# A fixed, periodic order of instructions in place of a list scheduler, with PSUM banks used by halves, in an attention and soft-MoE kernel

## The chip, the cores and the metric

The kernel runs on one core of a Trainium2 chip. The metric is the device time of one execution, in microseconds; below it is called the time. A profiled execution gives a trace beside its time: the instructions of TensorE (PE, with its weight loads apart as PEld), VectorE (DVE), ScalarE (ACT), GpSimd (POOL) and SyncE (SP, which only issues transfers here), and the transfers.

## What is computed

```python
def _attn_ref(q, kv, w_sr):                  # q [4, 12288, 128], kv [4, 384, 32, 128]
    kv_pool = kv.reshape(B, H // r, r, W // r, r, C).mean(axis=(2, 4))     # r = 4
    kv_flat = kv_pool.reshape(B, -1, C) @ w_sr                             # 768 keys a batch
    k = v = kv_flat
    s = scale * (q @ k.transpose(0, 2, 1))
    a = np.exp(s - s.max(-1, keepdims=True))
    a /= a.sum(-1, keepdims=True) + 1e-09
    return a @ v
def _moe_ref(x, phi, w1, w2):                # x [49152, 128], 8 experts, 4 slots each
    logits = x @ phi                         # 32 slots
    d = np.exp(logits - logits.max(0, keepdims=True))
    d /= d.sum(0, keepdims=True) + 1e-09     # over all tokens
    slot_input = d.T @ x
    for e in range(E):
        slot_out[e] = np.maximum(slot_input[e] @ w1[e], 0.0) @ w2[e]
    c = np.exp(logits - logits.max(1, keepdims=True))
    c /= c.sum(1, keepdims=True) + 1e-09     # over the slots
    return c @ slot_out
```

`_moe_ref` gets the output of `_attn_ref`, flattened to 49152 tokens.

## The kernel before

**Tiling.** A tile is 128 queries. There are 384 tiles, 96 to a batch, in 48 groups of eight (`G`). The attention output x is never made: the logits are P @ (v phi), and the slots' inputs are (D^T P) @ v, where P holds the exponentials of the scores and D the exponentials of the logits with a running maximum over the tokens.

**Per tile** (`plan_tile`): `qk` makes the scores with six matmuls (high and low parts of q and k), `rmax` (VectorE) the negated row maximum, `pexp` (ScalarE) the exponentials and their row sum. The last 384 of the 768 columns go to float16 as a high half (`p_hi`, ScalarE) and a low half (`p_lo`, GpSimd), and `p_dma` has them transposed by a transfer that SyncE issues. The first 384 columns of a pair of tiles are transposed by VectorE (`ptr`). Every four tiles `q_hi` (ScalarE) and `q_lo` (GpSimd) split q.

**Per group** (`plan_logits`, `plan_group`): `la_mm` (three steps, LA below) and `lb_mm` (three, LB) add up the logits in two PSUM tiles, `lp` and `lq`; two copies on ScalarE (`l_ev`) bring them to SBUF, `l_sel` multiplies them with a selecting matrix into `psl`, `l_tr` (VectorE) transposes them into LL, `l_n` (GpSimd) divides by the row sums. `m_col`, `m_mm`, `m_red`, `m_run` make the maximum over tokens (VectorE, TensorE, VectorE), `d_sub`, `d_exp`, `d_mul` (GpSimd, ScalarE, GpSimd) make D, `t_mm` (four steps of a pair of tiles, T0 to T3 below) makes D^T P in `pst`, and `t_acc` adds it up. `c_max`, `c_sub`, `c_exp` prepare the last softmax; `c_sum`, `c_eps`, `c_rec`, `c_mul` finish it, group by group.

**Per batch:** the keys of the next batch come in by one plain load of SyncE and three accumulating loads of GpSimd (`kv_acc`) and two folding transfers (`kv_fold`), into the tail of LL. `kv_ops` then makes k, u = v phi and v (`k_mm`, `u_mm`, `u_t`, `v_mm` on TensorE and what empties them); `b_tr`, `b_sum`, `b_mm`, `b_acc` close a batch.

**Tail:** the weights are loaded, the experts run (`e_psi` to `e_fin`), and 32 chunks of 12 tiles are transposed (`o_tr`), multiplied (`o_mm`), copied (`o_ev`) and written out (`o_dma`).

**What sets the order.** Every step is an `op` of a `Plan`, with an engine, a cost, a priority in assumed time (`T0`: 2 us a tile), what it depends on, and the rings of buffers that it takes and uses. `Plan.emit` runs a list scheduler at build time over those costs: at each step the engine that can start first takes its best ready operation (`NEAR`, `HOLD` and the flag `hot` shade the choice). The outcome is the program order of TensorE, VectorE, ScalarE and GpSimd; each engine then works strictly in that order, and waits where an operand is not there. PSUM holds three tiles of two banks in the ring `s` (scores; also `lq`, `pu`) and one tile of two banks in the ring `m`, which `lp`, `psl`, `pg`, `pst` and the small products take in turn, one at a time.

Of the kernel before, what the change touches and what calls it, by code (L numbers as in the profile page):

```python
# [24 lines left out]

class Plan:
    LAG = 0.08
    NEAR = 0.12
    HOLD = 0.7

    def __init__(self, rings):
        self.cap = rings
# [12 lines left out]

    def emit(self):
        ops = self.ops
        inf = math.inf
        waits = [len(o[4]) for o in ops]
        nexts = [[] for _ in ops]  # L50
        for n, o in enumerate(ops):
            for d in o[4]:
                nexts[d].append(n)
        ready, avail = {}, {}
        for n, o in enumerate(ops):
            avail.setdefault(o[0], [])
            ready[n] = o[8]
            if waits[n] == 0:
                avail[o[0]].append(n)
        left = {key: len(u) for key, u in self.users.items()}  # L60
        part, freed, rings = {}, {}, {}
        free = dict.fromkeys(avail, 0.0)
        todo = len(ops)

        def acquire(n):
            t = 0.0
            want = {}
            for key in ops[n][6]:
                ring = key[0]
                held = rings.get(ring, ())  # L70
                want[ring] = want.get(ring, 0) + 1
                back = self.cap[ring] - want[ring] + 1
                if len(held) >= back:
                    t = max(t, freed.get(held[-back], inf))
            return t

        def best(e):
            found = []
            for n in avail[e]:
                t = acquire(n)  # L80
                if t < inf:
                    found.append((max(free[e], ready[n], t), ops[n][3], n))
# [945 lines left out]
```

## Time and profile before

| | us |
|---|---|
| median of 3 runs | 1182.01 (1180.49 to 1182.15) |
| profiled execution, its own time | 1180.24 |
| its span, first to last instruction | 1178.5 |
| TensorE, VectorE, ScalarE, GpSimd busy | 896.4, 779.6, 736.6, 660.5 |

The span is what the trace covers; the execution's own time has 1.7 us more around it. Busy time counts an engine's instructions, and not its waits or the issue of transfers. The ends of matmuls are modelled, so a matmul's listed length is longer than the step from one start to the next. The granted clock of TensorE is given as a share of 2.4 GHz: 1.00 is that level, 0.50 is 1.2 GHz.

### The profile page before, as it was taken

The numbers are of one execution on the slowest core, as the hardware profiler recorded it, in microseconds if no ns is written. First come the engines' busy times: TensorE is split into PE (matmuls) and PEld (weight loads), VectorE is DVE, ScalarE is ACT, GpSimd is POOL, SyncE is SP. The second block draws the span as 40 slices with busy tenths as digits, with TensorE's granted clock in tenths as the row PEclk, the third lists the DMA queues.
The fourth block names the chain that finished last, engine by engine and source line by source line (L and its number), as shares of the span: only waits on it lengthen the run. The fifth ranks groups of instructions, "written<-read, shape, count | busy, mean of one in ns | idle before, by whom it ended". The sixth has DMA issues, their size and how long they took to land. (4 is left out here: it accounts for less than half of the span.)

```text
span 1178.5 us, 32165 instructions
## 1 busy us (share of the span) xinstructions
PE 896.4 (76%) x12708; PEld 674.6 (57%) x12708; DVE 779.6 (66%) x1629; ACT 736.6 (63%) x1548; POOL 660.5 (56%) x893
## 2 busy tenths in 40 slices
PE   1738988878970976898874398988897988985893
PEld 0627776556750764676653277765675766763341
DVE  5617778567831865878760468786885787784492
ACT  1626888567840864878761458785885788773251
POOL 1428677456742754777761557675775777774000
PEclk9969999889985997999997699999998999998895
DMA  7797777365797753566587646875773766759299
GB/s 298 153 177 120 119 127 119 63 111 95 129 186 141 121 98 66 102 122 121 113 171 150 127 72 118 115 128 83 115 123 75 122 118 116 121 82 304 94 412 379
DMA packets 332262, 165.18 MB, mean 140 GB/s; under 512 B 309968, under 2 KB 310224, under 8 KB 331216
## 3 DMA queue, kind: packets, MB, share of 16 engines
q1 hardware_dynamic: 328368, 145.29, 59.0%
q0 software_dynamic: 3312, 17.70, 8.0%
q8 instruction: 100, 1.64, 0.6%
q14 instruction: 50, 0.41, 0.1%
q10 hardware_dynamic: 432, 0.15, 0.0%
HBM read 58.87 MB, written 25.17 MB: 71 GB/s over the span
## 5 line engine op out<-in xcount | busy, mean ns | idle before, releaser
L428 ACT ACTIVATE p<-s,nm 128x768 f32<-128x768 f32 x384 | 341.2, 889 | 199.6 <-DVE nm L420 199.0
L419 DVE TENSOR_REDUCE nm<-s 128x1 f32<-128x768 f32 x384 | 363.7, 947 | 145.6 <-PE s L415 145.1
L438 POOL TENSOR_TENSOR hl<-p,hl 128x384 f16<-128x384 f32 x384 | 353.4, 930 | 82.6 <-ACT hl L435 78.1
L413 PE MATMUL s<-khi,qhi 128*128 128x384 f32 x768 | 284.8, 371 | 64.1 <-ACT p L428 63.5
L414 PE MATMUL s<-klo,qhi 128*128 128x384 f32 x768 | 261.3, 340 | 0.0
L415 PE MATMUL s<-khi,qlo 128*128 128x384 f32 x768 | 261.3, 340 | 0.0
L435 ACT ACTIVATE hl<-p 128x384 f16<-128x384 f32 x384 | 200.8, 523 | 55.7 <-DMA pb<-hl 37.5
L413 PEld LDWEIGHTS s<-khi,qhi 128*128 128x128 f32 x768 | 146.8, 191 | 117.5 <-ACT p L428 84.1
L588 PE MATMUL pst<-p,D 128*32 128x192 f32 x3072 | 157.1, 364 | 74.0 <-POOL D L573 65.6
L450 DVE STREAM_TRANSPOSE pa<-p 128x768 f32<-128x768 f32 x192 | 183.3, 955 | 12.9 <-ACT p L428 12.7
L588 PEld LDWEIGHTS pst<-p,D 128*32 128x32 f32 x3072 | 106.6, 122 | 122.0 <-POOL D L573 78.7
L414 PEld LDWEIGHTS s<-klo,qhi 128*128 128x128 f32 x768 | 147.3, 192 | 0.5 <-issue 0.5
L415 PEld LDWEIGHTS s<-khi,qlo 128*128 128x128 f32 x768 | 146.6, 191 | 0.0
L393 POOL TENSOR_TENSOR qlo<-q,qhi 128x512 fp32r<-128x512 f32 x96 | 123.5, 1287 | 30.7 <-ACT qhi L389 30.5
L521 POOL TENSOR_TENSOR LL<-LL,ri 128x256 f32<-128x256 f32 x48 | 29.9, 623 | 128.5 <-DVE LL L507 128.5
L475 PE MATMUL lq<-pa,vu 32*32 32x256 f32 x2304 | 98.3, 390 | 1.5 <-ACT p L428 1.5
L475 PE MATMUL lp<-pa,vu 32*32 32x256 f32 x2304 | 97.3, 390 | 0.5 <-DVE acc L599 0.5
L389 ACT ACTIVATE qhi<-q 128x512 fp32r<-128x512 f32 x96 | 60.0, 625 | 33.5 <-PE s L414 22.1
L533 PE MATMUL pg<-ident,cm 128*128 128x128 f32 x96 | 24.0, 334 | 74.3 <-DVE cm L528 58.7
L428 ACT ACTIVATION_READ_ACCUMULATOR p<-s,nm 128x1 f32 x384 | 73.5, 191 | 0.0
L420 DVE TENSOR_SCALAR nm<-nm 128x1 f32<-128x1 f32 x384 | 59.0, 154 | 13.2
L475 PEld LDWEIGHTS lp<-pa,vu 32*32 32x32 f32 x2304 | 51.2, 103 | 27.6 <-issue 10.5
(121 smaller groups left out, 960.8 us busy)
## 6 DMA issues: line engine op xcount, KB each, us to landing
q<-qT SPq DMA_DIRECT2D x96, 256.0 KB, 3.1
outT<-o SPq DMA_DIRECT2D x32, 768.0 KB, 13.4
LL<-kvT POOLq DMA_DIRECT2D x9, 1536.0 KB, 11.0
LL<-kv SPq DMA_DIRECT2D x8, 768.0 KB, 11.4
pb<-hl SPq DMA_TRANSPOSE x384, 2.8
LL<-kvT SPq DMA_DIRECT2D x3, 1536.0 KB, 7.2
w_pa<-w SPq DMA_DIRECT2D x2, 1536.0 KB, 9.5
w_pb<-w SPq DMA_DIRECT2D x2, 1536.0 KB, 10.0
```

The costliest lines, as they stand in the source:

```text
L389: nc.scalar.activation(qsp[i][0], src, AF.Copy)
L393: nc.gpsimd.tensor_tensor(out=lo, in0=src, in1=hi.bitcast(F32), op=ALU.subtract)
L413: nc.tensor.matmul(s, hi[:, qc], khi[:, k], start=True, stop=False)
L414: nc.tensor.matmul(s, hi[:, qc], klo[:, k], start=False, stop=False)
L415: nc.tensor.matmul(s, lo[:, qc], khi[:, k], start=False, stop=True)
L419: nc.vector.tensor_reduce(out=NM[t], in_=S[t][:, :, :HK], axis=XY, op=ALU.max, negate=True)
L428: nc.scalar.activation(PP[t // 2][:, t % 2, :].rearrange("p (h n) -> p h n", h=2), S[t][:, :, :HK], AF.Exp, bias=NM.pop(t), scale=1.0, acc ...
L435: nc.scalar.activation(HL[t][:, 0, :], PP[t // 2][:, t % 2, KA:], AF.Copy)
L438: nc.gpsimd.tensor_tensor(out=HL[t][:, 1, :], in0=PP[t // 2][:, t % 2, KA:], in1=HL[t][:, 0, :], op=ALU.subtract)
L450: nc.vector.transpose(out=PA[g][:, :, o : o + 2, :].rearrange("p n a i -> p a n i"), in_=PP[k][:, :, :KA].rearrange("p a (n j) -> p a n j" ...
L475: nc.tensor.matmul(lp(g, c, r), VU[b][rows, kb, :], PA[g][rows, kb, :, :], start=(k == 0), stop=False, skip_group_check=True)
L588: nc.tensor.matmul(d["pst"][c * Q32 : (c + 1) * Q32, :KW], d["D"][:, t, :], pp[:, u, c * KW : (c + 1) * KW], start=(t == 0), stop=(t == G ...
```

## The change

- `Plan` no longer schedules. Each operation has a kind; a table `TAU` gives each kind a time in units of a tile, counted from the start of its group (or of its batch, or of the drain), and the key of an operation is that start plus `TAU`, lifted to just after the keys of what it depends on. `emit` issues all operations sorted by key. So the order repeats every eight tiles.
- The ring `m` is gone. One PSUM tile `mt` of two banks stays for the whole kernel: the left halves (256 columns of each bank) take half of the logits, the right half of bank 0 takes `psl`, `pg` and the small products one after the other (`xs`), the right half of bank 1 takes `pst`. The other half of the logits stays in a tile of the ring `s`. In the sorted order T0 and T1 of a group stand before the next group's LA, T2 and T3 after it.
- The products for the keys (`pk`, `put`, `pv`) move to tiles of the ring `s`.
- The left half of the logits is copied by VectorE, the other by ScalarE.
- `p_hi` handles two tiles at a time; its ring holds three pairs instead of four tiles.
- The decay between running maxima gets operations of its own (`d_sa`, `d_xa`).
- `c_sum` and what follows are placed behind the loop; `c_eps` and `c_rec` take three groups at a time (`plan_c`).
- The folds of the keys add into the last quarter of the buffer instead of the first, and the products for v of a batch come some 22 tiles into that batch.

The order within one period, from the table modulo 8 (g is the group whose tiles are under way):

```
TensorE  s2 s3 | T0 T1 (g-2) | s4 s5 | LA LB (g-1) | s6 | l_sel (g-1) | s7 s0' | T2 T3 (g-2) | m_mm (g-1) | s1'
VectorE  m1 m2 m3 tr3 (g-1) tr0 m4 m5 r_inv tr1 l_ev-left d_al c_max m6 l_tr m7 m_col m0' t_acc m_red tr2
ScalarE  e0 d_exp e1 hi0 e2 e3 q_hi hi1 e4 e5 d_xa l_ev-right hi2 e6 q_hi e7 hi3 c_exp
GpSimd   lo6 (g-1) d_mul lo7 (g-1) d_sa r_eps lo0 lo1 q_lo lo2 lo3 lo4 l_n lo5 c_sub q_lo d_sub
```

(s, m, e, hi, lo, tr stand for `qk`, `rmax`, `pexp`, `p_hi`, `p_lo`, `ptr`; a prime marks the next group.)

```diff
+TAU = {
+    "hi0": -128.709, "bal": -112.015, "bsum": -91.792, "uout": -80.082, "humax": -75.029, "vout1": -65.577,
...
+    "s6": 4.627, "csum20": 4.65, "lo2": 4.848, "hi2": 4.933, "csum12": 5.084, "pd0": 5.176, "m6": 5.268, "lo3": 5.288,
...
+    "kf1": 7.979, "lo6": 8.223, "xh5": 8.397, "pd5": 8.491, "csum19": 8.658, "csum32": 8.676, "xpsi1": 8.69,
...
+    "LA2": 11.712, "cmul7": 11.906, "rinv": 12.048, "LB0": 12.066, "LB1": 12.253, "LB2": 12.44, "lev1": 12.739,
...
+    "cmul46": 14.728, "mmm": 15.347, "kv2": 15.59, "mred": 15.661, "ceps0": 15.831, "dsub": 15.889, "csum25": 15.947,
...
+    "uhl": 49.473, "kv1": 49.582, "crec10": 49.625, "csum29": 50.281, "khi1": 51.385, "ceps11": 51.407,
...
+    "kf0": 66.665, "khi0": 70.75, "csum43": 71.878, "ceps15": 75.948, "umm": 76.456, "umax": 77.26, "usc": 77.826,
...
+    def __init__(self):
         self.ops = []
-        self.log = []
-        self.users = {}
-
-    def op(self, eng, cost, prio, deps, fn, acq=(), use=(), lat=0.1, at=0.0, hot=False):
-        n = len(self.ops)
-        acq = [k for k in acq]
-        use = [k for k in use if k not in acq]
-        for key in acq + use:
-            self.users.setdefault(key, []).append(n)
-        self.ops.append((eng, cost, lat, prio, sorted(set(deps)), fn, acq, use, at, hot))
-        return n
+
+    def op(self, eng, kind, at, deps, fn, acq=(), use=()):
+        key = at + TAU.get(kind, 0.0)
+        for d in deps:
+            key = max(key, self.ops[d][2] + 1e-4)
+        self.ops.append((eng, kind, key, sorted(set(deps)), fn, list(acq), [k for k in use if k not in acq], at))
+        return len(self.ops) - 1
...
+        for n in sorted(range(len(self.ops)), key=lambda n: (self.ops[n][2], n)):
+            self.ops[n][4]()
...
-    CAP = {"s": 3, "m": 1, "p": 10, "pa": 2, "pb": 2, "hl": 4, "q": 4, "qs": 2, "lps": 1, "g": 3, "kv": 1, "K": 2, "V": 1}
+    CAP = {"s": 3, "l": 1, "x": 1, "T": 1, "p": 10, "pa": 2, "pb": 2, "hl": 3, "q": 4, "qs": 2, "lps": 1, "g": 3, "kv": 1, "K": 2, "V": 1}
...
+    mt = pm.tile([P, 2, 512], F32, tag="m", name="m")
+
+    def ss(name):
+        return ring(ps, "s", [P, 2, 512], name)
+
+    def xs(name):
+        return mt[:, 0, 256:]
...
         n = 2 - h
-        nc.gpsimd.dma_start(out=kvb[:, :n, :], in_=kvb[:, n : 2 * n, :], accum_op=ALU.add, max_dma_last_dim=4 * 2 * NK)
+        o = KVC - n
+        nc.gpsimd.dma_start(out=kvb[:, o:, :], in_=kvb[:, o - n : o, :], accum_op=ALU.add, max_dma_last_dim=4 * 2 * NK)
...
-    def p_hi(t):
-        HL[t] = ring(sp, "hl", [P, 2, NK - KA], f"hl_{t}", F16)
-        nc.scalar.activation(HL[t][:, 0, :], PP[t // 2][:, t % 2, KA:], AF.Copy)
+    def p_hi(k):
+        HL[k] = ring(sp, "hl", [P, 2, 2, NK - KA], f"hl_{k}", F16)
+        nc.scalar.activation(HL[k][:, :, 0, :], PP[k][:, :, KA:], AF.Copy)
...
-            GD[g]["lp"] = [ring(pm, "m", [P, 2, 512], f"lp_{g}"), ring(ps, "s", [P, 2, 512], f"lq_{g}")]
+            GD[g]["lps"] = ring(gp, "lps", [P, NQD, LW], f"lps_{g}")
+            lq = ss(f"lq_{g}")
+            GD[g]["lp"] = [mt[:, 0, :LW], mt[:, 1, :LW], lq[:, 0, :LW], lq[:, 1, :LW]]
+            GD[g]["lq"] = lq
...
-                    lp(g, c, r), VU[b][rows, kb, :], PA[g][rows, kb, :, :], start=(k == 0), stop=False, skip_group_check=True
+                    lp(g, c, r), VU[b][rows, kb, :], PA[g][rows, kb, :, :], start=(k == 0 and r != 1), stop=False, skip_group_check=True
...
-            d["lps"] = ring(gp, "lps", [P, NQD, LW], f"lps_{g}")
-        nc.scalar.activation(d["lps"][:, 2 * u : 2 * u + 2, :], d["lp"][u][:, :, :LW], AF.Copy)
+            nc.scalar.activation(d["lps"][:, 2:, :], d["lq"][:, :, :LW], AF.Copy)
+        else:
+            nc.vector.tensor_copy(d["lps"][:, :2, :], mt[:, :, :LW])
...
-            d["pst"] = ms(f"pst_{g}")
+            d["pst"] = mt[:, 1, 256:]
...
+    def d_sa(g):
+        d = GD[g]
...
+        ops["s", t] = op("PE", f"s{og}", at, need, lambda: qk(t), acq=[("s", t)], use=[("qs", i), ("K", b)])
+        ops["m", t] = op("DVE", f"m{og}", at, [ops["s", t]], lambda: rmax(t), use=[("s", t)])
...
+        ops["ph", k] = op("ACT", f"hi{kg}", at, [ops["e", t]], lambda: p_hi(k), acq=[("hl", k)], use=[("p", k)])
+        for v in range(2):
+            x = t - 1 + v
+            xo = og - 1 + v
+            lo = op("POOL", f"lo{xo}", at, [ops["ph", k]], lambda x=x: p_lo(x), use=[("hl", k), ("p", k)])
+            ops["pd", x] = op(
+                "SP", f"pd{xo}", at, [lo] + ([ops["pd", x - 1]] if x else []), lambda x=x: p_dma(x),
+                acq=[("pb", g)] if xo == 0 else [], use=[("hl", k), ("pb", g)],
             )
...
+        need = [ops["t", t // 2], ops["u", b]] + ([ops["T", g - 1]] if g else [])
...
+        e0 = op("ACT", "lev0", at, [a], lambda: l_ev(g, 0), use=[sl[1]] + lk)
+        e1 = op("DVE", "lev1", at, [a], lambda: l_ev(g, 1), use=[sl[0]] + lk)
...
+        sb = op("POOL", "dsub", at, [mr], lambda: d_sub(g), use=gk)
+        ex = op("ACT", "dexp", at, [sb], lambda: d_exp(g), use=gk)
+        a = op("POOL", "dmul", at, [ex, ri], lambda: d_mul(g), use=gk)
+        al = a
...
+            a = op("PE", f"T{pr}", at, [a], lambda pr=pr: t_mm(g, pr), acq=[mk] if pr == 0 else [], use=[mk, ("p", g * GP + pr)] + gk)
...
+            a = op("POOL", f"kv{c}", t, [a], lambda c=c: kv_acc(nb, c), use=[("kv", nb)])
+        f0 = op("POOL", "kf0", t, [a], lambda: kv_fold(nb, 0), use=[("kv", nb)])
+        f1 = op("POOL", "kf1", t, [f0], lambda: kv_fold(nb, 1), use=[("kv", nb)])
+        kv_ops(nb, t, [[f1], [f1]], [("kv", nb)])
...
+    def plan_c(k, at):
+        gs = range(k * CG, (k + 1) * CG)
+        a = [op("DVE", f"csum{g}", at, [ops["ce", g]], lambda g=g: c_sum(g)) for g in gs]
+        a = op("POOL", f"ceps{k}", at, a, lambda: c_eps(k))
+        a = op("DVE", f"crec{k}", at, [a], lambda: c_rec(k))
+        for g in gs:
+            ops["c", g] = op("POOL", f"cmul{g}", at, [a], lambda g=g: c_mul(g))
...
+    for k in range(NG // CG):
+        plan_c(k, DRAIN)
...
```

## Rows read from the trace of the kernel before

**Rows 1.** The page's part 1: busy time, share of the span, instructions of each engine.
```profile
PE 896.4 (76%) x12708; PEld 674.6 (57%) x12708; DVE 779.6 (66%) x1629; ACT 736.6 (63%) x1548; POOL 660.5 (56%) x893
```
**Rows 2.** Windows: stretch, its length, busy time by engine, granted clock, DMA share, GB/s.
```profile
905.20:923.20 18.00, 16.01 (x256) 12.75 (x255) 14.50 (x32) 14.53 (x32) 13.34 (x18) 1.00 0.67 118
...
941.20:959.20 18.00, 15.97 (x257) 12.71 (x255) 14.53 (x32) 14.41 (x32) 13.33 (x18) 1.00 0.70 124
```
**Rows 3.** TensorE's timeline, one group: start, length, operation [idle before, and what ended it].
```profile
943.61 0.46 PE L533 MATMUL pg<-ident,cm 128*128 128x128 f32 x2 [0.83 <-DVE cm L528]
...
947.35 2.81 PE L588 MATMUL pst<-p,D 128*32 128x192 f32 x64 [1.19 <-POOL D L573]
950.09 0.44 PE L413 MATMUL s<-khi,qhi 128*128 128x384 f32 x1
...
952.37 0.45 PE L475 MATMUL lp<-pa,vu 32*32 32x256 f32 x8
...
955.52 0.44 PE L413 MATMUL s<-khi,qhi 128*128 128x384 f32 x1
...
957.83 0.64 PE L502 MATMUL psl<-lps,selb 128*32 128x256 f32 x8
...
965.32 2.81 PE L588 MATMUL pst<-p,D 128*32 128x192 f32 x64 [1.15 <-POOL D L573]
```
**Rows 4.** ScalarE's timeline: the first and the last of the 384 exponentials.
```profile
34.07 0.90 ACT L428 ACTIVATE p<-s,nm 128x768 f32<-128x768 f32 x1 [0.81 <-DVE nm L420]
...
1069.02 0.88 ACT L428 ACTIVATE p<-s,nm 128x768 f32<-128x768 f32 x1
```
**Rows 5.** Waits, GpSimd for its own transfers: us in total, times, longest.
```profile
POOL LL L273 <- DMA LL<-kvT: 56.3, 6, 10.1
...
POOL LL L279 <- DMA LL<-kvT: 27.0, 3, 9.9
...
POOL LL L279 <- DMA LL<-LL: 15.2, 3, 5.2
```
**Rows 6.** Groups by form: shapes, count | busy us, mean ns | idle before, releasers.
```profile
L972 DVE COPY o<-po 128x768 f32<-128x768 f32 x32 | 29.9, 933 | 8.0 <-DMA outT<-o 2.7 <-ACT o L970 2.6 <-PE po L962 2.6
L941 POOL TENSOR_TENSOR LL<-LL,RM 128x256 f32<-128x256 f32 x48 | 29.6, 616 | 4.9 <-DVE RM L938 4.9
...
L930 DVE TENSOR_REDUCE RM<-LL 128x8 f32<-128x256 f32 x48 | 19.7, 411 | 18.8 <-ACT LL L610 18.7
...
L597 DVE COPY acc<-pst 128x192 f32<-128x192 f32 x4 | 1.4, 358 | 8.1 <-PE pst L588 8.1
```
**Rows 7.** GpSimd's timeline, the same group: subtraction, a low half, product of D.
```profile
944.90 0.74 POOL L554 TENSOR_TENSOR D<-LL,gm 128x256 f32<-128x256 f32 x1 [0.61 <-DVE gm L548]
...
945.82 0.91 POOL L438 TENSOR_TENSOR hl<-p,hl 128x384 f16<-128x384 f32 x1
946.69 0.61 POOL L573 TENSOR_TENSOR D<-D,ri 128x256 f32<-128x256 f32 x1
```
**Rows 8.** Transposes' landing, clean stretch 936:990, then all; accumulating loads, KB, us to landing.
```profile
DMA to landing us min/median/max: 2.7/3.4/4.5
...
DMA to landing us min/median/max: 2.7/2.8/11.3
...
LL<-kvT POOLq DMA_DIRECT2D x9, 1536.0 KB, 11.0
```
**Rows 9.** Groups by form: key, u and v matmuls of the three batches in the loop.
```profile
L287 PE MATMUL pk<-LL,w_sb 128*128 128x384 f32 x12 | 7.1, 684 | 0.8 <-DVE gm L538 0.8
L348 PE MATMUL pv<-w_sb,LL 128*96 128x128 f32 x48 | 6.2, 272 | 0.0
...
L303 PE MATMUL pu<-LL,wp 128*128 128x384 f32 x12 | 5.7, 606 | 0.0
```
**Rows 10.** TensorE's first output matmul (timeline); the output phase (windows).
```profile
1111.22 6.62 PE L962 MATMUL po<-ct,sl 32*128 32x384 f32 x36 [0.46 <-ACT sl L891]
...
1120.00:1178.50 58.50, 37.05 (x210) 16.04 (x208) 34.70 (x50) 21.88 (x27) 0.00 (x0) 0.75 0.97 396
```

More of the change, by code (lines that the diff above doesn't have):

```diff
@@ L23 @@
 Q32 = 32
-class Plan:
[L27 to L32, printed above, removed]
-        self.ops = []
-        self.log = []
-        self.users = {}
-    def op(self, eng, cost, prio, deps, fn, acq=(), use=(), lat=0.1, at=0.0, hot=False):
-        n = len(self.ops)
-        acq = [k for k in acq]
-        use = [k for k in use if k not in acq]
-        for key in acq + use:
-            self.users.setdefault(key, []).append(n)
-        self.ops.append((eng, cost, lat, prio, sorted(set(deps)), fn, acq, use, at, hot))
-        return n
-    def emit(self):
[L47 to L82, printed above, removed]
-            if not found:
-                return None
-            t0 = min(found)[0] + self.NEAR
-            hot = [f for f in found if ops[f[2]][9]]
-            if hot:
-                h = min(hot)
-                if h[0] - t0 < self.HOLD:
-                    fits = [(p, t, n) for t, p, n in found if t <= t0 and t + ops[n][1] <= h[0] + 0.1]
-                    return min(fits) if fits else (h[1], h[0], h[2])
-            return min((p, t, n) for t, p, n in found if t <= t0)
-        end = 0.0
-        while todo:
-            picks = [(c[1], e, c[2]) for e in avail if (c := best(e)) is not None]
-            if not picks:
-                raise RuntimeError("the plan is stuck: " + str([(e, [(ops[n][3], ops[n][6]) for n in avail[e]][:8]) for e in avail]))
-            t, e, n = min(picks)
-            eng, cost, lat, prio, deps, fn, acq, use, at, hot = ops[n]
-            avail[e].remove(n)
-            free[e] = t + cost
-            done = t + cost + lat
-            self.log.append((t, cost, e, n))
-            end = max(end, done)
-            todo -= 1
-            for key in acq:
-                rings.setdefault(key[0], []).append(key)
-            for key in acq + use:
-                left[key] -= 1
-                part[key] = max(part.get(key, 0.0), done)
-                if left[key] == 0:
-                    freed[key] = part[key] + self.LAG
-            for d in nexts[n]:
-                waits[d] -= 1
-                ready[d] = max(ready[d], done + self.LAG if ops[d][0] != e else t + cost + (0.0 if e == "PE" else 0.05))
-                if waits[d] == 0:
-                    avail[ops[d][0]].append(d)
-            fn()
-        self.end = end
@@ L254, in attention_then_soft_moe @@
     ops = {}
-    ops["q", 0] = op("SP", 0.3, -300, [], lambda: q_load(0), acq=[("q", 0)], lat=6.0)
+    ops["q", 0] = op("SP", "qd0", -90, [], lambda: q_load(0), acq=[("q", 0)])
     pool0 = {}
-    at = 5.0
+    lds = {}
+    for h in range(2):
+        for a0 in range(0, R2, 4):
+            lds[h, a0] = op("SP", "hld", -89, [], lambda h=h, a0=a0: ld0(h, a0, 4))
     for h in range(2):
@@ L299, in u_mm @@
     def u_mm(b):
-        D["pu", b] = ring(ps, "s", [P, 2, 512], f"pu_{b}")
-        D["put", b] = ms(f"put_{b}")
+        D["pu", b] = ss(f"pu_{b}")
         for h in range(2):
@@ L817, in attention_then_soft_moe @@
         key = (tag, ("w", k))
[L818 removed]
+        prev = [op("SP", "wl", DRAIN + 8 + 0.1 * k, prev, lambda which=which, u0=u0, n=n, tag=tag, k=k: w_load(w1 if which == 1 else w2, w1s if which == 1 else w2s, u0, n, tag, k), acq=[key])]
         wl[which].append(prev[0])
```

334 lines of the change are left out of this document (146 added, 188 removed), and 36 rows, old and new, of the table TAU.

## The prediction

> **What bounds the kernel now.** I read in this order: the busy table of the page, the windows of stretches without disturbance, TensorE's timeline over one group of eight tiles, the timeline of the chain that makes D, the table of waits, and the head and tail.
>
> No engine is full over the whole span; TensorE has the most, 76% [rows 1]. In an undisturbed stretch it is different: 16.0 of 18 us on TensorE, 14.5 on VectorE and on ScalarE, 13.3 on GpSimd, at granted clock 1.00 [rows 2]. One group there takes from D^T P to D^T P 965.32 - 947.35 = 17.97 us [rows 3]. In it TensorE is idle twice: 0.83 us before the group's maximum (it waits for VectorE's column maximum) and 1.19 us before D^T P (it waits for GpSimd's D) [rows 3]. 17.97 - 0.83 - 1.19 = 15.95 us is what TensorE itself needs for a group: the undisturbed loop is near TensorE's floor, with some 2 us per group to win.
>
> But the loop is not undisturbed. Its 384 exponentials start between 34.07 and 1069.02 us [rows 4]. That is 47 whole groups and the 7 tiles of the last, about 7/8 of a period more, so 47.9 periods; at 17.97 they would take 860 us, and they take 1035. So 175 us lie in stalls. Of these GpSimd's waits for its own accumulating loads are the part that the table names: 56.3 + 27.0 + 15.2 = 98.5 us, in three batches 32.8 us each [rows 5]. GpSimd's queue holds the low halves of P and q and all of D, so while it waits for a load the other engines run dry. The other 77 us or so are groups that the emitted order itself stretches, and the key operations of three batches.
>
> **The period after.** The list scheduler is replaced by one fixed sequence with a period of eight tiles, and I read that sequence from the table modulo 8. On TensorE it is: s2 s3, T0 T1, s4 s5, the logits LA LB, s6, the selecting matmuls, s7 s0, T2 T3, the maximum, s1. Three loops have to close within one period:
> - TensorE: 15.95 us from above. The figure counts the modelled tail of the last matmul before each idle stretch, some 0.2 us each; splitting D^T P in two blocks adds a change of kind, about 0.1. Floor 15.6 to 16.1.
> - VectorE: 14.5 us [rows 2]. The c sum (0.41 [rows 6]) leaves the loop; the copy of half the logits (128x512 out of PSUM) comes. No such copy is in the trace: 128x192 takes 0.36 and 128x768 takes 0.93 us [rows 6]; between them by size, 0.68, which is also the slope of the two. 14.5 - 0.41 + 0.68 = 14.8 us, under TensorE's floor.
> - The chain that crosses engines: selecting matmuls to D^T P takes 965.32 - 957.83 = 7.49 us [rows 3]; in it GpSimd already puts one low half of P between the subtraction and the product of D [rows 7], as the new order does. Then T0 and T1 (half of 950.09 - 947.35 = 2.74, so 1.37), two tiles of scores (952.37 - 950.09 = 2.28), the logits (955.52 - 952.37 = 3.15) [rows 3], and s6 with its change of kind (half of 2.28, 1.14), beside which the copy (0.68) lies. Sum 15.4 us.
>
> So three loops at 15.6 to 16.1, 14.8 and 15.4 us, and all engines in strict order. A late hand-over in one delays the others and is not made good by picking another instruction. I add 0.2 to the middle of TensorE's floor and take **16.1 us** a group; the bounds are 15.6 (its lower end, no stall) and 16.9 (nearly half of the two present idle stretches remains).
>
> ScalarE loses one of two logit copies and makes the high halves of two tiles at once; at 14.5 us it was not the bound, so I book that at nothing. GpSimd loses the c product (0.62 [rows 6]) from its 13.3 us [rows 2] and keeps over 3 us of slack. The three-pair ring for the high and low halves holds six tiles instead of four: nothing, as long as transposes land in time. The last one has 4.9 us: lo7 follows the product of D, takes 0.9 (945.82 to 946.69) after the product's 0.6 and so ends 0.8 after T0's start, which is 0.66 behind the product's [rows 3, 7]; LB0 comes 1.37 + 2.28 + two thirds of 3.15, 5.7 us, after T0's start. In the clean stretch a transpose lands in 3.4 us [rows 8].
>
> **A rule that speaks against the change.** Its rows first: the copy of the left halves takes up to 0.93 us [rows 6], a half of D^T P 1.37 us [rows 3], and in the new order T2 T3 stand behind s7 and s0, that is some 2 us after the selecting matmuls that themselves wait for the copy. So TensorE writes no right half while VectorE reads a left one, and I book nothing.
> The Trainium skill, "PSUM — Partial Sum Buffer", section "PSUM bank collisions raise a hardware error", says that two engines must not be in one bank and quadrant at a time even at different columns, and advises a guard by bank rather than by address. No row here shows a bank in two parts; what such a guard would cost if the order slips is the second rival.
>
> **Batches.** Per batch the key operations cost TensorE at most (7.1 + 5.7 + 6.2) / 3 = 6.3 us for keys, u and v [rows 9], and some 1 us for transposes and the batch sum: 7 us, since the loop is TensorE's. They move from the pool of one-bank tiles into the scores' ring of three. On GpSimd's queue the table keeps two waits of four: the second accumulating load stands directly behind the first, the second fold directly behind the first (their own times in the table lie before those of what they depend on, so they are lifted to it). Queued behind are epsilon, low halves, qlo and ln, and behind these the transposes, TensorE's next scores and the logits. Price by present waits: 56.3 / 6 + 15.2 / 3 = 9.4 + 5.1 = 14.5 us of blocked GpSimd per batch [rows 5]; its slack takes a little, I book 12 (9 to 14.5). The third load and the first fold have 7.4 and 9.7 tile slots, 15 and 19 us, after their predecessors, which land in 11.0 us [rows 8]: nothing, or up to 9.4 + 9.0 us if the landing doubles beside the transposes. For that, and for the strict order around the keys, I add 5 (0 to 15). Sum 24 us a batch (16 to 36), three batches 72 us (48 to 108).
>
> **Head and tail.** First exponential at 34.1 us [rows 4]; the first batch's v matmuls now stand ahead of the first scores, so +4: 38. The first two groups lack logits or D^T P and run ahead of the period: -5. From the last exponential to the end 1178.5 - 1069.0 = 109.5 us. The output starts at 1111.2 and its DMA share is 0.97 to the end [rows 10]. The c sums and products that move there are 48 x 0.41 on VectorE and 48 x 0.62 on GpSimd [rows 6], 20 and 30 us. Of VectorE's share all but some eleven stand ahead of the first output chunk, where it waits for the expert matmuls; the rest fall into a phase where VectorE is busy for 34.7 of 58 us and GpSimd for 0.0 [rows 10]. The cover is the output DMA and the expert chain: +2 (0 to 10, should VectorE become what feeds the DMA).
>
> **The sum.** 38 - 5 + 47 x 16.1 (757) + 7/8 of a period to the last exponential (14) + 72 + 109.5 + 2 = 987 us of span. The profiled execution's own time is 1180.2 for a span of 1178.5 and the runs shown have a median of 1182.0, so 3.5 lie between span and median: **990 us**, 16% under the time before. Low end: 15.6 a group and 48 for batches, 990 - 24 - 24 = 942; a little under it for a shorter head, 935. High end of this case: 16.9 and 108, 990 + 38 + 36 = 1064.
>
> **Rivals.**
> - Hand-overs eat the gain: the order is fixed, so the present 2 us of idle time on TensorE stay under other names. Then 17.5 a group: 990 + 47 x 1.4 = 1056 us. For it: three loops within 1.3 us of each other. Against it: the new order puts other work into each of the two idle stretches. 0.20.
> - The shared banks make the halves exclude each other: D^T P falls behind the copy, and each group pays what it pays now ahead of D^T P, 1.2 us: 990 + 56 = 1046. It is also the case in which the change does not overlap what it says. Against it: the 2 us of distance. 0.07.
> - Slower than before: the last pair's low half stands behind D's subtraction and product on GpSimd, so its transpose starts late, and LB0 waits for it in every period. LB0 suffers from a landing of 4.9 us on, as worked out above; each us of landing beyond costs one per group, and it decides against the change from (1182 - 990) / 47 = 4.1 us more, that is a steady landing beyond 9.0 us: at 11 us 990 + 47 x 6.1 = 1277. The longest landing of the present run is 11.3 [rows 8], but the median is 2.8 and the DMA engines are busy for 0.67 to 0.70 of a period [rows 2], which is 0.75 to 0.78 of one of 16.1 us. 0.04.
>
> Forecast case 0.67, rivals 0.20, 0.07, 0.04, and 0.02 for a result near no change. Faster by over 0.2% 0.94, within 0.2% 0.01, slower 0.05 (0.2% is about what a measurement of this kernel can tell from no change). The range 935 to 1064 takes in the forecast case and the first two rivals, less their ends.
>
> **What would show it.** Right: in the middle of a batch D^T P's first halves follow each other at 15.6 to 16.9 us; TensorE's idle time before the group's maximum and before T0 is under 0.3 us together; GpSimd's table of waits has two waits for loads per batch instead of four; ScalarE's wait for VectorE shrinks most; no c sums before the last groups; the output DMA share stays at 0.97. Wrong: if TensorE's first score of a pair waits for an exponential in every group (scores' ring), if LB waits for a transposed tile, if VectorE is over 0.95 busy (then it is the floor), or if the last exponential to the end takes over 120 us.

## The result and the profile after

The changed kernel takes 1033.3 us (median of 4 runs, 1025.1 to 1037.0) against 1182.1 in the runs beside it: ratio 0.873, 95% interval 0.868 to 0.879. That lies inside the range 935 to 1064, 43 us above the forecast of 990. The profiled execution took 1037.0 us for a span of 1035.3. Medians and ratios leave out an execution that is over 1.5% above the fastest of its kernel; below this concerns one execution of the quarters.

The page's first part, then VectorE's timeline (two additions of D^T P one group apart, and between them the new copy of the left logits), then the windows of two undisturbed groups, then ScalarE's first and last exponential:

```profile
PE 897.7 (87%) x12708; PEld 669.5 (65%) x12708; DVE 803.9 (78%) x1645; ACT 677.6 (65%) x1308; POOL 652.5 (63%) x861
```
```profile
807.94 0.42 DVE L567 SCALAR_TENSOR_TENSOR acc<-acc,al,m 128x192 f32<-128x192 f32 x1 [0.16 <-PE m L496]
...
818.18 0.69 DVE L459 COPY lps<-m 128x512 f32<-128x512 f32 x1 [0.59 <-PE lq L449]
...
824.13 0.41 DVE L567 SCALAR_TENSOR_TENSOR acc<-acc,al,m 128x192 f32<-128x192 f32 x1 [0.15 <-PE m L496]
```
```profile
808.00:824.20 16.20, 16.09 (x256) 12.68 (x255) 14.68 (x31) 13.24 (x27) 12.56 (x17) 1.00 0.77 132
840.40:856.60 16.20, 16.10 (x256) 12.64 (x255) 14.74 (x31) 13.14 (x27) 12.52 (x17) 1.00 0.91 148
```
```profile
37.04 0.90 ACT L386 ACTIVATE p<-s,nm 128x768 f32<-128x768 f32 x1 [2.34 <-DVE nm L378]
...
919.57 0.90 ACT L386 ACTIVATE p<-s,nm 128x768 f32<-128x768 f32 x1 [0.82 <-DVE nm L378]
```

An undisturbed group takes 824.13 - 807.94 = 16.19 us (17.97 before [rows 3]), and TensorE is busy for 16.09 of 16.20; the two idle stretches of before are gone. From the first to the last exponential it is 882.5 us instead of 1035 [rows 4]. 47.9 periods of 16.18 are 775, so 107.5 us of stalls are left of 175. The gain there, 152.5 us, is thus 85 from the period (47.9 x 1.79) and 67.5 from fewer stalls. The head gives back 3 us and the tail 6.2 (115.7 after the last exponential, 109.5 before): 143 us of span.

**Where the stalls are.** The waits of GpSimd for its own accumulating loads (us in total, times, longest), which stood at 56.3, 27.0 and 15.2 [rows 5]; and waits for transposed high and low halves of P:

```profile
POOL LL L234 <- DMA LL<-kvT: 34.1, 3, 11.6
POOL LL L241 <- DMA LL<-LL: 20.6, 3, 7.3
...
PE m L449 <- DMA pb<-hl: 25.5, 7, 7.5
ACT hl L393 <- DMA pb<-hl: 18.5, 5, 5.2
```

GpSimd's share fell from 98.5 to 54.7 us, with two waits a batch, as the table has it. The third row hardly stood in the trace of before: TensorE's LB waits for transposes, six times in groups around the loads and folds and once, for 4.4 us, in the tail. I measured each group of batch 1 between additions of D^T P and took 16.18 from it. Windows of these groups, the columns as in [rows 2]:

```profile
127.08:153.98 26.90, 17.85 (x256) 13.93 (x255) 14.63 (x31) 12.76 (x26) 14.51 (x19) 0.81 0.77 145
153.98:183.42 29.44, 20.98 (x256) 15.61 (x255) 14.87 (x31) 13.72 (x27) 14.15 (x18) 0.77 0.97 173
183.42:205.07 21.65, 18.62 (x255) 13.80 (x254) 14.76 (x30) 14.02 (x29) 13.52 (x19) 0.86 0.70 140
205.07:223.81 18.74, 18.41 (x263) 14.10 (x263) 16.73 (x37) 13.53 (x26) 13.22 (x17) 0.98 0.91 136
223.81:242.85 19.04, 17.97 (x260) 13.07 (x259) 15.59 (x32) 13.95 (x29) 12.21 (x16) 1.00 0.60 104
```

The excess is 10.7 (wait for a load), 13.3, 5.5 (wait for a fold), 2.6 and 2.9 us (the products for the keys); the group that changes batches adds 4.2. Some 39 us for batch 1, 37 and 37.5 for the others. The largest is a group in which GpSimd waits for no transfer at all. GpSimd's timeline shows what is in it (L234 issues the accumulating loads, L397 is a low half, L241 a fold):

```profile
144.24 1.20 POOL L234 DMA_DIRECT2D LL<-kvT  x1 [11.58 <-DMA LL<-kvT]
...
159.88 1.23 POOL L234 DMA_DIRECT2D LL<-kvT  x1
...
177.96 0.92 POOL L397 TENSOR_TENSOR hl<-p,hl 128x384 f16<-128x384 f32 x1 [10.76 <-ACT hl L393]
...
195.99 0.88 POOL L241 DMA_DIRECT2D LL<-LL  x1 [7.29 <-DMA LL<-LL]
```

The third load is issued at 159.88. SyncE's queue, on which the transposes stand, then works like this (three transposes there, and four in an undisturbed stretch); under it all transposes of 158 to 176 us, with the time that one issue took and the time to landing:

```profile
160.86 11.99 SPq L403 DMA_TRANSPOSE pb<-hl  x3
...
833.94 7.64 SPq L403 DMA_TRANSPOSE pb<-hl  x4
```
```profile
L403 SPq DMA_TRANSPOSE pb<-hl x7: 1215/1237/7543, 157.6 to 174.8; - x7
...
DMA to landing us min/median/max: 2.8/5.2/12.6
```

One issue of a transpose took 7.54 us instead of 1.24, and one landing 12.6. TensorE in that group:

```profile
159.00 0.69 PE L371 MATMUL s<-khi,qhi 128*128 128x384 f32 x1 [2.93 <-ACT p L386]
...
174.31 0.40 PE L449 MATMUL m<-pb,vb 128*32 128x256 f16 x2 [5.53 <-DMA pb<-hl]
```
```profile
172.00:174.00 2.00, 0.00 (x0) 0.00 (x0) 0.00 (x0) 0.00 (x0) 0.00 (x0) 0.50 1.05 177
...
176.00:178.00 2.00, 2.00 (x13) 1.65 (x6) 1.11 (x3) 1.33 (x2) 0.04 (x1) 0.50 1.46 90
```

Of the 13.3 us, 8.46 are TensorE idle. 2.93 of it is a wait for an exponential that stood behind a high half, and that high half had waited 3.91 us for a transpose to free its buffer; 5.53 is LB. The other 4.9 us are TensorE busy for longer (20.98 against 16.09): its granted clock fell to 0.50, the 1.2 GHz level, while it stood idle, and stayed there over the first instructions after. So the wait for a transfer is paid a second time at the lower clock. (The wait of 2.93 us ends before the third load is issued, so it belongs to what went before.)

### The profile page after: what moved, and what is told of

It is laid out like the page before. It is cut to its first block, busy times and chain, and to the rows that moved or that the text cites. A ratio compares the mean times of both kernels' runs of the same rounds, so it can differ in the third digit from the quotient of the medians.

```text
span 1035.3 us, 31658 instructions
## 1 busy us (share of the span) xinstructions
PE 897.7 (87%) x12708; PEld 669.5 (65%) x12708; DVE 803.9 (78%) x1645; ACT 677.6 (65%) x1308; POOL 652.5 (63%) x861
## 4 chain that ended last, share of the span: by engine, by line
PE 60%; POOL 12%; DMA 9%; DVE 7%; issue 4%; ACT 2%; POOLq 0%; ACTq 0%; DVEq 0%
PE m L556 11%; PE s L371 10%; PE s L373 7%; PE s L372 7%; DMA pb<-hl 6%; PE m L437 5%; POOL hl L397 4%; PE po L929 4%; DMA LL<-kvT 4%; PE m L449 3%; POOL D L517 3%; PE m L465 3%; POOL D L541 2%; PE lq L437 2%; PE lq L449 2%
## 5 line engine op out<-in xcount | busy, mean ns | idle before, releaser
L397 POOL TENSOR_TENSOR hl<-p,hl 128x384 f16<-128x384 f32 x384 | 359.1, 971 | 130.2 <-ACT hl L393 69.5
L386 ACT ACTIVATE p<-s,nm 128x768 f32<-128x768 f32 x384 | 343.8, 897 | 139.2 <-DVE nm L378 130.4
L377 DVE TENSOR_REDUCE nm<-s 128x1 f32<-128x768 f32 x384 | 362.3, 944 | 47.9 <-PE s L373 43.4
L393 ACT ACTIVATE hl<-p 128x768 f16<-128x768 f32 x192 | 161.2, 839 | 23.7 <-DMA pb<-hl 18.5
L556 PE MATMUL m<-p,D 128*32 128x192 f32 x3072 | 152.8, 342 | 15.3 <-POOL D L541 10.2
L351 POOL TENSOR_TENSOR qlo<-q,qhi 128x512 fp32r<-128x512 f32 x96 | 128.2, 1335 | 32.5 <-ACT qhi L347 32.5
L556 PEld LDWEIGHTS m<-p,D 128*32 128x32 f32 x3072 | 93.8, 114 | 65.2 <-POOL D L541 26.3
L437 PE MATMUL m<-pa,vu 32*32 32x256 f32 x2304 | 96.8, 389 | 0.0
L449 PE MATMUL m<-pb,vb 128*32 128x256 f16 x864 | 60.0, 286 | 25.6 <-DMA pb<-hl 25.5
L459 DVE COPY lps<-m 128x512 f32<-128x512 f32 x48 | 33.1, 689 | 58.4 <-PE lq L449 58.3
L449 PEld LDWEIGHTS <-vb 128*32 128x32 f16 x1728 | 43.7, 100 | 49.3 <-issue 39.1
L437 PEld LDWEIGHTS m<-pa,vu 32*32 32x32 f32 x2304 | 52.8, 103 | 28.4 <-issue 11.2
## 6 DMA issues: line engine op xcount, KB each, us to landing
LL<-kvT POOLq DMA_DIRECT2D x9, 1536.0 KB, 12.3
```

What stands on the lines that cost most here:

```text
L351: nc.gpsimd.tensor_tensor(out=lo, in0=src, in1=hi.bitcast(F32), op=ALU.subtract)
L377: nc.vector.tensor_reduce(out=NM[t], in_=S[t][:, :, :HK], axis=XY, op=ALU.max, negate=True)
L386: nc.scalar.activation(PP[t // 2][:, t % 2, :].rearrange("p (h n) -> p h n", h=2), S[t][:, :, :HK], AF.Exp, bias=NM.pop(t), scale=1.0, acc ...
L393: nc.scalar.activation(HL[k][:, :, 0, :], PP[k][:, :, KA:], AF.Copy)
L397: nc.gpsimd.tensor_tensor(out=hl[:, 1, :], in0=PP[t // 2][:, t % 2, KA:], in1=hl[:, 0, :], op=ALU.subtract)
L437: nc.tensor.matmul(lp(g, c, r), VU[b][rows, kb, :], PA[g][rows, kb, :, :], start=(k == 0 and r != 1), stop=False, skip_group_check=True)
```

## The experiments

Two theories for what the batches cost beyond the forecast. *Queue*: GpSimd is blocked by dependent loads, and the groups after it work off its backlog. *Contention*: an accumulating load slows the transposes while it is in flight, wherever it stands. Beside them stand the questions of what sets the period and where the tail's 6 us come from. The runs without the third load, with only the plain load, without the third score matmul, with the left copy on ScalarE, with T2 and T3 joined and with the c sums in the loop are one execution each, and the changed kernel's own executions spread over 12 us; from these runs single groups count for more than totals.

**Loads and folds moved so far apart that GpSimd waits for none.**

```diff
-"kv0": 34.314, "kv1": 49.582, "kv2": 15.59, "kf1": 7.979
+"kv0": 26.314, "kv1": 41.582, "kv2": 49.582, "kf1": 71.3
```

> Only the places of the key transfers in the order change: the plain load and the first accumulating load move 8 tiles earlier, the second accumulating load takes the place that the first had, and the second fold stands 4.6 tiles behind the first instead of directly behind it. The changed kernel loses 39 us in each of three batches against its period of 16.18: 10.7 in the group with the wait of the second load (11.6 us of blocked GpSimd), 13.3 in the group of the third load (where GpSimd does not wait for it), 5.5 with the wait of the second fold (7.3), 9.6 in the key groups. Theory 1 (blocked queue: the 13.3 are the backlog of transposes left by the 10.7): the waits fall to near 0 and all but the key groups goes, 3 x (10.7 + 13.3 + 5.5) = 88 us off, or 70 to 88: about 945 to 965. Theory 2 (contention: an accumulating load beside the transposes costs some 13 us wherever it stands): each of the two loads that now run without a wait costs 13, so only the fold's 5.5 a batch goes: 1010 to 1025.

Measured 1011.9 us (ratio 0.857, 0.854 to 0.861), where contention had put it. GpSimd's waits for loads are gone, and the loads still cost 17.8 us in batch 1 and 24 in batch 2, in the groups in which one is in flight. TensorE's timeline there:

```profile
368.49 0.40 PE L449 MATMUL m<-pb,vb 128*32 128x256 f16 x2 [7.68 <-DMA pb<-hl]
...
395.18 0.40 PE L449 MATMUL m<-pb,vb 128*32 128x256 f16 x2 [8.52 <-DMA pb<-hl]
```

The blocked queue is worth about 21 us of 1033; what the loads still cost, they cost without it.

**No third load.**

```diff
-        for c in range(1, R2 // KVC):
+        for c in range(1, R2 // KVC - 1):
```

> The third accumulating load of each batch is left out, so a quarter of the keys' pixels is missing from the mean. Theory 1 (the 13.3 us in its group are the backlog from the wait before it): that group still loses 8 to 13 us, time 1015 to 1033. Theory 2 (they are contention of this load with the transposes): that group falls to 16.2 to 18 us, 3 x 12 = 36 us off, about 995.

Measured 1010.8, outside both expectations. The group in which the third load stood loses 3.5 to 6.5 us instead of 12.9 to 13.4: 7 to 9 us of it came with that load, the rest stands without it, behind the wait before. All of LB's waits for transposes shrink from 25.5 to this:

```profile
  PE m L449: 7.8, 3
```

**Only the plain load, no accumulating loads and no folds.**

```diff
-        for c in range(1, R2 // KVC):
+        for c in range(1, 1):
...
-        f0 = op("POOL", "kf0", t, [a], lambda: kv_fold(nb, 0), use=[("kv", nb)])
-        f1 = op("POOL", "kf1", t, [f0], lambda: kv_fold(nb, 1), use=[("kv", nb)])
+        PO[nb] = kvb[:, KVC - 1, :]
+        f1 = a
```

> All accumulating loads and folds of the later batches are left out (the keys of batches 1 to 3 are made of one of sixteen pixels); the plain load and the key operations stay. If GpSimd's transfers (waits and contention together) are what the batches cost above the key operations: 3 x (10.7 + 13.3 + 5.5) = 88 us off: 945 (935 to 955). If the key operations in strict order cost part of the 29.5: 960 to 1000.

Measured 946.3, 87 us less than the changed kernel, 29 a batch. What remains of a batch is 9.6 us in the groups with key products. TensorE's busy time over the whole span drops from 897.7 to 874.0 with the same number of matmuls:

```profile
PE 874.0 (93%) x12708; PEld 656.2 (69%) x12708; DVE 802.4 (85%) x1645; ACT 676.8 (72%) x1308; POOL 637.1 (67%) x846
```

Group by group, some 20 of these 24 us lie in the three batches' groups around the loads and folds, where the changed kernel's granted clock is mostly 0.77 to 0.92 and this run's is 1.00; the rest lies in head and drain. So about 20 of the 87 us are the lower clock, most of the rest idle time.

**The third score matmul left out**, to see whether TensorE sets the period.

```diff
-            nc.tensor.matmul(s, hi[:, qc], klo[:, k], start=False, stop=False)
-            nc.tensor.matmul(s, lo[:, qc], khi[:, k], start=False, stop=True)
+            nc.tensor.matmul(s, hi[:, qc], klo[:, k], start=False, stop=True)
```

> The third of the three score matmuls (low part of q with high part of k) is left out, two matmuls of 0.17 us a tile, 2.8 us of TensorE per group. If TensorE's floor sets the period of 16.18, the period falls until the next loop holds it: the chain across engines, which holds one tile of scores on its way three times over (s4, s5, s6: 1.0 us less), 15.4 - 1.0 = 14.4, or VectorE at 14.8: 14.6 to 15.3 us a group, 40 to 70 us off in all. If VectorE or hand-overs set it, it stays within 0.2 us of 16.18 and the time within 10 us.

Measured 999.2. Two additions of D^T P on VectorE, the window between them, and a wait of LB in the group of batch 3's third load:

```profile
795.08 0.41 DVE L566 SCALAR_TENSOR_TENSOR acc<-acc,al,m 128x192 f32<-128x192 f32 x1
810.03 0.41 DVE L566 SCALAR_TENSOR_TENSOR acc<-acc,al,m 128x192 f32<-128x192 f32 x1
```
```profile
795.08:810.03 14.95, 13.79 (x240) 9.69 (x240) 14.44 (x32) 13.07 (x27) 12.56 (x17) 1.00 0.95 151
```
```profile
622.26 0.40 PE L448 MATMUL m<-pb,vb 128*32 128x256 f16 x2 [20.31 <-DMA pb<-hl]
```

The period is 14.95 us: TensorE is what set 16.18. Its busy time in a group falls by 2.3 us, from 16.09 to 13.79 (the expectation had 2.8), and the period by 1.24. TensorE now stands idle for 1.16 us of it, 0.55 for an exponential and 0.61 for D, and VectorE is busy for 14.44 of 14.95. Whether VectorE or the chain across engines holds the period there is not separated. In all the run took 34 us less, not the 40 to 70 expected: the group with the wait of 20.31 us took 42.6 us, 29.5 in the changed kernel.

**The left copy given to ScalarE.**

```diff
-            nc.vector.tensor_copy(d["lps"][:, :2, :], mt[:, :, :LW])
+            nc.scalar.activation(d["lps"][:, :2, :], mt[:, :, :LW], AF.Copy)
...
-        e1 = op("DVE", "lev1", at, [a], lambda: l_ev(g, 1), use=[sl[0]] + lk)
+        e1 = op("ACT", "lev1", at, [a], lambda: l_ev(g, 1), use=[sl[0]] + lk)
```

> The copy of the left halves of the logits goes back to ScalarE, ahead of the other copy there. VectorE gets 0.69 us a group less, ScalarE 0.5 more, and the selecting matmuls' operands are ready some 0.3 us later. If TensorE's floor sets the period: unchanged within 0.1 us, time within 6 us of the changed kernel. If VectorE sets it: 0.5 to 0.7 us a group less, 25 to 33 us off. If the chain across engines sets it: 0.3 to 0.5 us a group more, 15 to 25 us on.

Measured 1031.2, and the period stays: 837.40 - 821.22 = 16.18.

```profile
821.22 0.41 DVE L567 SCALAR_TENSOR_TENSOR acc<-acc,al,m 128x192 f32<-128x192 f32 x1 [0.15 <-PE m L496]
837.40 0.41 DVE L567 SCALAR_TENSOR_TENSOR acc<-acc,al,m 128x192 f32<-128x192 f32 x1 [0.15 <-PE m L496]
```

VectorE is not the floor, and it does not matter here which engine copies.

**T2 and T3 joined to T0 and T1**, so that D^T P no longer stands around the logits.

```diff
-"T2": 22.538, "T3": 22.942
+"T2": 17.7, "T3": 17.8
```

> T2 and T3 move in the order to directly behind T0 and T1, so the whole of D^T P stands in one block ahead of s4 and of the next logits; nothing of it lies behind the logits. If only TensorE's sum counts: 16.1 to 16.2 a group, time within 6 us. If the split is what lets the other engines work on (s4 comes 1.4 us later, and the maxima and exponentials of s4 and s5 with it, while s1 comes earlier): 0.5 to 1.4 us a group more, 25 to 65 us on: 1058 to 1098.

Measured 1080.4. TensorE's timeline, D^T P in one piece, and the matmul of the group's maximum:

```profile
837.44 2.81 PE L556 MATMUL m<-p,D 128*32 128x192 f32 x64 [0.18 <-POOL D L541]
...
850.57 0.49 PE L496 MATMUL m<-ident,cm 128*128 128x128 f32 x2 [0.74 <-DVE cm L491]
...
854.72 2.81 PE L556 MATMUL m<-p,D 128*32 128x192 f32 x64 [0.17 <-POOL D L541]
```

The period is 854.72 - 837.44 = 17.28 here, 17.24 in most groups: 1.06 more than 16.18, or 50 us over 47 groups. The idle stretch ahead of the maximum is back, at 0.74 us (0.83 before [rows 3]). Two steps of D^T P were what covered it.

**The c sums back in the loop**, group by group.

```diff
-    CG = 3
+    CG = 1
...
-        a = [op("DVE", f"csum{g}", at, [ops["ce", g]], lambda g=g: c_sum(g)) for g in gs]
+        a = [op("DVE", "zs", at + 36.06, [ops["ce", g]], lambda g=g: c_sum(g)) for g in gs]
...
-        plan_c(k, DRAIN)
+        plan_c(k, k * G)
```

> The c sums, epsilons, reciprocals and products go back into the loop, one group at a time, some 36 tiles behind their group. VectorE gets 0.6 us a group more (14.7 to 15.3 of 16.18), GpSimd 0.85 more (12.5 to 13.4). If TensorE's floor keeps the period: 16.18 to 16.3 a group, and the stretch from the last exponential to the end (115.7 us in the changed kernel, 109.5 in the one before) shortens by the 3 to 6 us that the sums behind the loop cost there: 1024 to 1036 in all. If hand-overs have no slack for more work on VectorE: 0.4 to 0.6 us a group more, 1045 to 1060.

Measured 1046.9. A window of one undisturbed group:

```profile
832.40:848.60 16.20, 16.07 (x256) 12.61 (x256) 15.06 (x34) 13.23 (x26) 13.37 (x19) 1.00 0.87 133
```

VectorE has 15.06 us of work instead of 14.68, and the period stays at 16.18 to 16.21. After the last exponential it is 113.7 us, 2 less. Against the profiled execution of the changed kernel it is 9.9 us more, and this lies in the groups with loads of batch 3: the third load's takes 36.4 us, 29.5 in the changed kernel. This was one execution, and these groups differ from one execution to the next, so what the c sums do to the total stays open. That the time came out near one of the expected figures does not bear that branch out, since its cause (a longer period) is not there.

**Accumulating loads in quarters, spread evenly.** Each of the three loads becomes four of 384 KB, 1.9 to 3.9 tiles apart; the plain load moves to 24.314, the folds to 63.4 and 71.4.

```diff
+    def kv_piece(b, c, x):
+        nc.gpsimd.dma_start(
+            out=kvb[:, x : x + 1, :], in_=kvT[b - 1, :, c * KVC + x : c * KVC + x + 1, :], accum_op=ALU.add, max_dma_last_dim=4 * 2 * NK
+        )
...
+        PIECE = [29.5, 31.4, 33.62, 37.5, 39.4, 41.62, 45.5, 47.4, 49.62, 53.5, 55.4, 57.62]
+        last4 = {x: a for x in range(KVC)}
+        for n, at in enumerate(PIECE):
+            c, x = n // KVC + 1, n % KVC
+            last4[x] = op("POOL", "kvp", t + at, [last4[x]], lambda c=c, x=x: kv_piece(nb, c, x), use=[("kv", nb)])
+        f0 = op("POOL", "kf0", t, list(last4.values()), lambda: kv_fold(nb, 0), use=[("kv", nb)])
```

> Each accumulating load is cut into four of 384 KB, each with a place of its own in GpSimd's order some 2 to 4 tiles behind the one ahead (the plain load moves 10 tiles earlier, the folds stand a whole period apart); the same bytes move and GpSimd waits for none. With whole loads so placed, a batch still loses 18 to 24 us around them. If a burst delays a transpose by up to its own time and the period has some 1.5 us of slack for that (4.9 us to LB0 against 3.4 of landing), bursts of 3 us cost next to nothing: under 6 us a batch, 960 to 975. If it is the share of the DMA engines that is short (the same bytes beside the same transposes): 18 us a batch remain, 1005 to 1015.

Measured 967.7 us (four executions, 961.6 to 970.1), ratio 0.818 (0.815 to 0.822): faster than both kernels, and inside the first expectation. The profiled execution is a fifth, of 988.2 us, so only single durations are read from it, and its longest waits may be what sets it apart. The landing (KB each, median us to landing), and the longest wait of LB:

```profile
LL<-kvT POOLq DMA_DIRECT2D x36, 384.0 KB, 5.9
...
pb<-hl SPq DMA_TRANSPOSE x384, 3.8
```
```profile
333.19 0.40 PE L454 MATMUL m<-pb,vb 128*32 128x256 f16 x2 [12.44 <-DMA pb<-hl]
```

A whole load lands in 12.3 us in the changed kernel (11.0 before [rows 8]), a quarter in 5.9, not in the 3 that the expectation reckoned with. The wait of 12.4 us stands where two pieces had been issued 4.3 us apart, at 311.54 and 315.86. Eleven pairs of pieces stand 4.3 us apart in this trace and only this one has such a wait, so the distance alone does not explain it. SyncE then needed this for four transposes:

```profile
315.67 15.43 SPq L408 DMA_TRANSPOSE pb<-hl  x4
```

**Whole loads placed just behind LB**, so that they are in flight while no logits wait for a transpose.

```diff
-"kv0": 34.314, "kv1": 49.582, "kv2": 15.59, "kv3": 57.012, "kf0": 66.665, "kf1": 7.979
+"kv0": 28.2, "kv1": 36.2, "kv2": 44.2, "kv3": 52.2, "kf0": 60.2, "kf1": 68.2
```

> Whole accumulating loads again, without waits of GpSimd, but each at the place in the period that follows the start of LB (mod 4.2 tiles; in the kernel with loads moved apart it was 1.0 to 1.6, just ahead of the last pair's transposes, and LB then waited 5.5 to 8.5 us for them). The plain load stands at 28.2, loads at 36.2, 44.2, 52.2, folds at 60.2 and 68.2. If it is the place against the last pair's transposes that makes a load dear: a load that starts after LB has some 12 us, its own length, before the next last pair, so under 6 us a batch above the key operations: 950 to 975. If the load's bytes or its overlap with any transposes cost: as with the loads moved apart, 1005 to 1017.

Measured 992.6 (0.841, 0.838 to 0.845), between the two expectations. LB waits for a transpose only once, near the end. But the wait moved:

```profile
ACT hl L393 <- DMA pb<-hl: 38.2, 13, 6.3
```

The transposes that are late now hold the ring of three pairs, and ScalarE's next high half waits for them, with its exponentials behind. Groups with loads still cost 11.4 to 15.7 us a batch. Against the loads moved apart, the place takes the price from 21.9 to 15.4 us a batch (time above 946.3) and does not remove it.

**Quarters, three per period, just behind LB** (the plain load at 23.5, the folds at 60.2 and 68.2).

```diff
+        PIECE = [28.2, 28.9, 29.5, 36.2, 36.9, 37.5, 44.2, 44.9, 45.5, 52.2, 52.9, 53.5]
```

> Quarter loads, three to a period, at 4.2 to 5.5 tiles in the period (28.2, 28.9, 29.5, then the same 8, 16 and 24 tiles later), all behind the start of LB and ahead of the next last pair; plain load at 23.5, folds at 60.2 and 68.2. If the place against the last pair's transposes decides: under 4 us a batch above the key operations, 948 to 962. If two quarters in flight at once beside the transposes are what slows these (in the first run of quarters LB waited up to 12.4 us where two pieces were issued 4.3 us apart): 965 to 990.

Measured 991.5 (0.842, 0.839 to 0.845), 24 us above the spread quarters and just above the second expectation. Landing, and the waits for transposes:

```profile
LL<-kvT POOLq DMA_DIRECT2D x36, 384.0 KB, 7.5
```
```profile
PE m L454 <- DMA pb<-hl: 13.8, 7, 5.4
ACT hl L398 <- DMA pb<-hl: 22.8, 12, 5.4
```

A piece lands in 7.5 us here and in 5.9 when spread, which fits pieces in flight together slowing each other. That they slow the transposes more is not shown: these land in 3.9 us (3.8 when spread), and the only trace of the spread quarters is that of their slowest execution. By the times it is the spread that helps, more than the place; the plain load and the folds also stand elsewhere in the two runs, which no run separates. Counted as time above 946.3 (one execution), per batch, the loads cost 29.0 us as the change has them, 21.9 apart, 15.4 behind LB, 15.1 in clustered quarters and 7.1 in spread quarters.

## Why the prediction came out as it did, point by point

**The period: right.** 16.1 forecast, 16.18 measured, on the engine named. TensorE needs 16.0 to 16.1 of it (floor 15.6 to 16.1, so at its upper end), and VectorE 14.7 (14.8). The left copy takes 689 ns (680, which is right between the two rows but is not their slope: that is 1.0 ns a column, 0.51 us for 512). The run without the third score matmul and the two that move VectorE's work show TensorE as the floor. The chain at 15.4 us was no bound; that run went below it, with less TensorE work in the chain too, so its size was not measured. The first rival (hand-overs keep the 2 us idle) is out: 0.1 us of idle time is left in a group of 16.20. One of the signs failed: ScalarE's wait for VectorE did not shrink most. It went from 199.0 to 130.4 us; GpSimd's wait for the transposed logits went from 128.5 to 36.0.

**The shared banks: right.** D^T P and the logits overlap as said, and the run with T2 and T3 joined prices it: 1.06 us a group. Where I cited the Trainium skill ("PSUM — Partial Sum Buffer", section "PSUM bank collisions raise a hardware error"), the period shows no price for a guard by bank. In the trace of the changed kernel no read of the shared tile overlaps a write to it, so the rule itself is not tested here.

**The batches: the step that failed.** 24 us each forecast, with 36 as upper bound; about 38 measured. Of the 114 us for three, 42 are above the forecast and that is nearly the whole miss. By terms: the two waits of GpSimd 10.7 + 5.5 = 16.2 for 12 (bound 14.5); key products and the change of batch 9.6 for 7; and "For that, and for the strict order around the keys, I add 5 (0 to 15)" measured 13.3, near its upper end. Two sentences beside it fell:
- "The three-pair ring ... nothing, as long as transposes land in time." They did not around the loads: ScalarE's high halves waited 18.5 us in 5 stretches, three of them beside an accumulating load and two around the folds. The sign stood in the trace of before, where I did not weigh it. Its view of the transposed tiles shows who waited for buffers that transposes held (us, times):

```profile
  ACT hl L435: 37.5, 14
...
  PE lp L487: 2.5, 1
```

- The slower rival was priced as a steady landing beyond 4.9 us in every group. Its mechanism is real, but only beside loads: in the undisturbed stretch 808 to 860 the median landing is 3.6 us (3.4 before [rows 8]) and the longest, 6.1, holds up no LB; beside a load they reach 12.6, and LB waited 25.5 us in 7 stretches, 21.1 of it around the loads and folds (2.5 in one before). The text had named this sign, LB waiting for a transposed tile, among what would make it wrong. I gave it as all or nothing and left its partial case out of the sum.

A third omission: no term for the clock. After the two waits in the group above TensorE worked at the 0.50 level, which cost 4.9 of its 13.3 us; over the groups around loads and folds it is about 20 us.

**Head, fill, tail.** First exponential 37.0 (38). The fill gave 6.5 (5): 775 + 114 - 882.5. The tail lost 6.2 (2, at most 10): 4.9 of it lies before the first output matmul, which comes 966.67 - 919.57 = 47.1 us after the last exponential, 42.2 before [rows 4, 10]. By the trace it is of the same kind: the last LB waits 4.36 us for transposes that share SyncE's queue with the weight loads, in a window with the DMA engines full (share 1.09). No run tried it, but accumulating loads are not needed for it: the run with only the plain load has such a wait too, of 5.2 us. The wait, the first output matmul, and the windows of the drain and the output:

```profile
934.17 0.40 PE L449 MATMUL m<-pb,vb 128*32 128x256 f16 x2 [4.36 <-DMA pb<-hl]
...
966.67 3.98 PE L929 MATMUL po<-ct,sl 32*128 32x384 f32 x20 [0.46 <-ACT sl L856]
```
```profile
919.60:940.00 20.40, 11.10 (x196) 5.89 (x196) 8.73 (x25) 3.40 (x8) 7.24 (x14) 0.66 1.09 333
975.00:1035.30 60.30, 46.04 (x220) 22.87 (x220) 41.72 (x68) 22.71 (x28) 17.66 (x34) 0.60 0.95 387
```

The c sums, which I had booked as the tail's only loss at 2, cost about 2 by the run that has them in the loop. The output phase keeps its DMA share, 0.95.

**The sum.** From first to last exponential 882.5 for 838: 4 from the period, 42 from the batches, less 1.5 from the fill. Tail 4 more, head 1 less: about 48 us between the profiled span and the forecast one, 43 between median and forecast. The time lies in the range because the other terms came out close; the batches alone, 114 for 48 to 108, left theirs.

**What stays open.** That accumulating loads slow the transposes is shown by taking them away, moving them and cutting them. How they do it in the DMA engines is not: the profile shows longer issues on SyncE's queue and a DMA share above 1 at little traffic (1.46 at 90 GB/s in the window at 176 us), and no run separates the two. Nor does a run tell whether it is the adding, the issue by GpSimd or the bytes alone. The plain load of the same 1536 KB, which SyncE issues at 540.87 us in the trace of the changed kernel, costs nothing that shows: the transposes around it land within 4.3 us, its group takes 20.44 us (20.43 at the next change of batch, which has no such load) and the next one 16.12. But it stands in the transposes' own queue and in a pause of theirs, so this is no like comparison.

## What to carry to other kernels

The fixed periodic order reached the floor of its fullest engine here, and that floor could be read beforehand as busy time per period. Like the order before it, it cannot step around a late transfer, so price the disturbed groups apart, with every transfer that shares the DMA engines, every ring that a late one holds, and the clock that TensorE loses while it waits. Large accumulating transfers beside small ones on which an engine depends were best cut and spread over the periods; here that was worth another 65 us.
